# A linear-attention block beside a bilinear feed-forward: four tiles centred first and scaled late, and another order of loads

## The chip, the cores and the metric

The kernel runs on one core of one Trainium2 chip. A core has five engines that run their own instruction queues in order and meet through semaphores: TensorE (PE, matrix products), VectorE (DVE), ScalarE (ACT), GpSimd (POOL) and SyncE (SP, which here only issues DMA). The metric is device time of one execution in microseconds, the median of several runs.

## The reference

The input x has 2048 rows of 512. Each row is normalised without learned parameters, and two branches read the result. Branch A is linear attention with 32 heads of 16: the feature map of queries and keys is the softmax of a per-head 16x16 projection, joined with the softmax of its negative. Branch B multiplies two projections elementwise and projects back. Everything is bfloat16.

```python
xn = (x - mean(x)) / sqrt(var(x) + 1e-5)
q, k, v = heads(xn @ wqkv)
pq, pk = q @ w_phi[h], k @ w_phi[h]              # 16 x 16 for each head
phi = lambda p: concat([softmax(p), softmax(-p)])
kv, z = phi(pk).T @ v, sum_s phi(pk)
o = (phi(pq) @ kv) / (phi(pq) @ z + 1e-6)
A = concat_heads(o) @ wo
B = ((xn @ w_gate) * (xn @ w_up)) @ w_down
out = x + A + B
```

## The kernel before

The 2048 rows are 16 tiles of 128 (index t), the 512 columns four quarters (q), the 1792 hidden columns 14 tiles (ft), and the rows of the feed-forward four groups of 512 (g).

The kernel doesn't write instructions directly. It records steps, each with its engine, what it reads and writes, and an estimated cost; `_order` then simulates the engines with these costs and lays down the order of each engine's queue, and `_emit_all` puts in the semaphore waits. For a DMA the recorded `at` is the time at which its landing is assumed. Steps marked `urgent` go ahead of others that could start at nearly the same time. So a changed cost or `at` may move any later instruction on any engine.

What is recorded, in order:

- Loads, all issued from SP's queue (line 165; transposing loads line 164): x tiles 0, 1, then 2-3 together; wv, the value part of wqkv; x tiles 4-7; the first four hidden tiles of w_gate and of w_up (`load_gu`, each 512 KB); w_phi; the key part of wqkv transposed (`load_wT(1)`); x tiles 8-15; the rest of the weights.
- 46 matmuls of zeros into PSUM bank 7, which wait for no load (line 369).
- For tiles 0 to 3 one after the other, `ln(t, 1)` and `k_pe(t)`. `ln` takes statistics of the tile (DVE, lines 413 and 415), adds epsilon (line 420, on DVE for the first four tiles, on POOL after) and raises to -0.5 on POOL (line 422); `emit_xn` subtracts the mean and scales (DVE, line 437), and for tiles below 8 transposes the tile with four 128x128 matmuls, which ACT copies out of PSUM into xnT. Tiles 8 to 15 are transposed by DMA. `k_pe` multiplies xnT with wv (a group of four 128x512 matmuls, "value group"), and ACT copies the result to vext.
- `make_wbd` spreads w_phi to block-diagonal form on POOL (line 395); `wprime(1)` multiplies it with the transposed key weights, 16 matmuls of 128x128, into the folded weights Wp.
- Then tiles in fours: `k_pk` (four matmuls with Wp, "key group") and `emit_exp`: ACT copies the scores and their negative side by side (1024 columns), DVE takes a tree of maxima (line 477) and subtracts (483), ACT exponentiates; `k_norm` sums on DVE (497) and normalises (521, 524). Between them go units of the feed-forward, `glu(g, ft)`: a gate group, an up group, ACT copies the gate, DVE multiplies (line 548) into hT. An up group reuses a PSUM bank that an earlier unit's DVE product must have read, and a gate group one that ACT must have read; with three banks the two kinds alternate.
- `emit_kv` multiplies keys and values; then the query side (`q_pk`, `q_scale`, `q_T`, `q_num`; `q_num` divides on DVE, line 618); and `final(t)`, 18 matmuls of 128x512 for the output tile, to which DVE adds x (line 645) before it is stored.

The helpers `mms` (line 297, all matmuls) and `act_op` (line 277, all ACT work) record for all others, so many different operations share those two lines.

Of the kernel before, what the change touches and what calls it, by code (L numbers as in the profile page):

```python
# [20 lines left out]
NQ = D // 128  # L21
# [176 lines left out]
def _build(nc, es, A_x, A_wqkv, A_w_phi, A_wo, B_w_gate, B_w_up, B_w_down, out):  # L198
# [93 lines left out]
    def mms(items, prio=None, warm=False):  # L292

        def fn(e):
            ins = None
            for o, l, r, a, z in items:
                ins = e.matmul(o, lhsT=l, rhs=r, start=a, stop=z)  # L297
            return ins
        reads = []
        writes = []  # L300
        c = 0.0
        for o, l, r, a, z in items:
            reads += [l, r]
            writes.append(o)
            c += max(25.0, o.free_size() / 2.4 + 2.3) * (1.6 if warm else 1.0)
        return sc.step(PE, fn, reads=reads, writes=writes, cost=c, lat=260.0, prio=prio)
# [33 lines left out]
    def load_w(on, dst, src, at, issue=500.0):  # L340
        return sc.dma(on, dst, src, at=at, issue=issue)
# [5 lines left out]
    def load_gu(on, f0, n, at):  # L347
# [4 lines left out]
    load_x(SP, 0, 1, 3150.0)  # L352
    load_x(SP, 1, 1, 3700.0)
    load_x(SP, 2, 2, 4800.0)
    load_w(SP, wv_v, A_wqkv[:, 1024:1536].rearrange("(q p) j -> p q j", p=128), 6800.0)
    load_x(SP, 4, 4, 8200.0)
    load_gu(SP, 0, 4, 10800.0)
    sc.dma(SP, wphi_v, bass.AP(tensor=A_w_phi.tensor, offset=A_w_phi.offset, ap=[[16, 128], [2048, NQ], [1, 16]]),
           at=12500.0)
    load_wT(1, 14500.0)  # L360
    load_x(SP, 8, 8, 17000.0)
# [7 lines left out]
    mms([(bank(7, 0, 128), zero, zero, True, True)] * 46, warm=True)  # L369
# [39 lines left out]

    def emit_ln_stats(t0, n):  # L410
# [3 lines left out]
        for t in range(t0, t0 + n):  # L414
# [4 lines left out]
        add = dve if t0 < 4 else pool  # L419
        add(lambda e: e.tensor_scalar(out=veps.unsqueeze(2), in0=var4, scalar1=1e-5, scalar2=None, op0=ALU.add),  # L420
            [mv_v[:, ts, :]], [veps], n)
# [13 lines left out]

    def emit_xn(t):
# [7 lines left out]
        b = next_a()  # L444
        mms([(bank(b, q * 128, 128), xn_tile(t)[:, q * 128:(q + 1) * 128], ident, True, True) for q in range(NQ)])
        act_op(xnT_v[:, :, t * 128:(t + 1) * 128], bank(b).rearrange("p (q s) -> p q s", q=NQ))
# [17 lines left out]
    def emit_exp(src_bank, e_out):  # L464
# [5 lines left out]
        act_op(pst[:, 0:512], bank(src_bank))  # L470
        act_op(pst[:, 512:1024], bank(src_bank), scale=-1.0)
# [35 lines left out]
    def k_pe(t):  # L507
        b = next_a()
        mms(group(bank(b), [(xnT(q, t * 128, 128), wv_v[:, q, :]) for q in range(NQ)]))
        act_op(vext_all[:, t, :, 0:64], bank(b).rearrange("p (c j) -> p c j", c=8))  # L510

    def k_pk(t):
        b = next_a()
        mms(group(bank(b), [(xnT(q, t * 128, 128), Wp_v[:, 1, q, :]) for q in range(NQ)]))
        p_slot["k", t] = emit_exp(b, ek_v[:, t, :])
# [74 lines left out]
    def q_pk(t):  # L590
        b = next_q()
        mms(group(bank(b), [(xnT(q, t * 128, 128), Wp_v[:, 0, q, :]) for q in range(NQ)]))
        p_slot["q", t] = emit_exp(b, eq(t))
# [18 lines left out]
    def q_num(t):  # L612
# [5 lines left out]
        dve(lambda e: e.tensor_tensor(  # L618
            out=o.rearrange("p (g h d) -> p g h d", g=8, h=4),
            in0=nd[:, :, 0:64].rearrange("p g (h d) -> p g h d", h=4),  # L620
            in1=w[:, :, :, None].to_broadcast([128, 8, 4, 16]), op=ALU.mult),
            [nd[:, :, 0:64], w], [o], 512)
# [8 lines left out]
    def final(t, b, cols=(0, 512)):  # L631
# [13 lines left out]
        dve(lambda e: e.tensor_tensor(out=og, in0=ob, in1=xs, op=ALU.add), [ob, xs], [og], c1 - c0, prio=-2.0)  # L645
# [17 lines left out]
    for t in range(4):  # L663
        first = len(sc.steps)
        ln(t, 1)
        for st in sc.steps[first:]:
            st.urgent = True
        k_pe(t)
    make_wbd()
    wprime(1)  # L670
# [191 lines left out]
```

## Time and profile before

| | us |
|---|---|
| median of three runs (223.28 to 223.78) | 223.43 |
| profiled execution | 222.97 |
| its span, first to last instruction | 221.2 |
| PE busy | 215.5 |
| DVE busy | 191.8 |
| ACT busy | 116.1 |
| POOL busy | 9.1 |
| matmuls of zeros and tile 0's transposes, in a row | 1.04 to 5.74 |
| PE idle before tile 1's transposes; before tile 3's | 0.72; 0.44 |
| first transposing load on SP's queue, issue | 5.19 to 11.11 |
| tiles 8-15 used first on DVE | 17.39 |

A row of the timeline gives start and length, engine, line, operation and shapes, how many instructions were merged into it (x), and in brackets the idle time of the engine before it with what ended that. A matmul's recorded length (some 380 ns for 512 columns) includes its run through the array; the next one starts before it has ended, so the pace is read from how many start in a stretch. About one matmul record in fifty is missing. Times below are in microseconds from the start of the span.

### The profile page before, as it was taken

The numbers are of one execution on the slowest core, as the hardware profiler recorded it, in microseconds if no ns is written. First come the engines' busy times: TensorE is split into PE (matmuls) and PEld (weight loads), VectorE is DVE, ScalarE is ACT, GpSimd is POOL, SyncE is SP. The second block draws the span as 40 slices with busy tenths as digits, with TensorE's granted clock in tenths as the row PEclk, the third lists the DMA queues.
The fourth block names the chain that finished last, engine by engine and source line by source line (L and its number), as shares of the span: only waits on it lengthen the run. The fifth ranks groups of instructions, "written<-read, shape, count | busy, mean of one in ns | idle before, by whom it ended". The sixth has DMA issues, their size and how long they took to land.

```text
span 221.2 us, 3597 instructions
## 1 busy us (share of the span) xinstructions
PE 215.5 (97%) x1288; PEld 107.1 (48%) x1312; DVE 191.8 (87%) x552; ACT 116.1 (52%) x193; POOL 9.1 (4%) x25
## 2 busy tenths in 40 slices
PE   8799999999999999999999999999999999999995
PEld 8355444444455454444464445444445444445444
DVE  5858999999992899999998999999999999985121
ACT  2769977684535999655527855646643331300000
POOL 4252000000020000000000000000000000000000
PEclk9999999999999999999999999999999999999999
DMA  5999941300005400000000044464245546745201
GB/s 172 328 281 401 357 128 28 71 0 0 0 9 91 95 3 0 0 0 3 0 1 3 0 82 84 49 139 77 53 94 118 119 98 101 160 94 123 71 24 49
DMA packets 44210, 19.39 MB, mean 88 GB/s; under 512 B 35232, under 2 KB 43168, under 8 KB 44192
## 3 DMA queue, kind: packets, MB, share of 16 engines
q1 hardware_dynamic: 44192, 19.16, 35.7%
q8 instruction: 10, 0.16, 0.3%
q14 instruction: 8, 0.07, 0.1%
HBM read 8.67 MB, written 2.10 MB: 49 GB/s over the span
## 4 chain that ended last, share of the span: by engine, by line
PE 73%; DVE 16%; SPq 4%; DMA 3%; issue 2%
PE ps L297 73%; DVE arena L548 4%; DVE arena L497 3%; DMA arena<-in_A_x_dram 3%; SPq L164 3%; DVE arena L477 3%; SPq L165 2%; DVE arena L413 2%; DVE arena L483 2%; DVE arena L521 1%; DVE arena L524 1%; DVE arena L437 0%; DVE arena L645 0%; DVE arena L415 0%
## 5 line engine op out<-in xcount | busy, mean ns | idle before, releaser
L297 PE MATMUL ps<-arena 128*128 128x512 bf16 (+4 forms) x1288 | 215.5, 328 | 3.5 <-DVE arena L368 1.0
L297 PEld LDWEIGHTS ps<-arena 128*128 128x128 bf16 x1312 | 107.1, 99 | 111.7 <-DVE arena L420 1.3
L277 ACT ACTIVATE arena<-ps 128x512 bf16<-128x512 f32 (+1 forms) x160 | 84.6, 596 | 47.3 <-PE ps L297 44.1
L277 ACT ACTIVATE arena<-arena 128x1024 bf16<-128x1024 bf16 x32 | 34.1, 1069 | 29.3 <-DVE arena L483 28.8
L497 DVE TENSOR_TENSOR arena<-arena 128x256 f32<-128x256 f32 (+3 forms) x128 | 48.8, 392 | 0.1
L548 DVE TENSOR_TENSOR arena<-ps,arena 128x512 bf16<-128x512 f32 x56 | 37.7, 674 | 2.8 <-ACT arena L277 1.4
L477 DVE TENSOR_TENSOR arena<-arena 128x256 bf16<-128x256 bf16 (+3 forms) x128 | 30.6, 267 | 2.9 <-ACT arena L277 2.8
L645 DVE TENSOR_TENSOR arena<-ps,arena 128x512 bf16<-128x512 f32 (+2 forms) x17 | 11.1, 655 | 13.8 <-PE ps L297 13.7
L483 DVE TENSOR_TENSOR arena<-arena 128x1024 bf16<-128x1024 bf16 x32 | 21.5, 671 | 0.0
L413 DVE BATCH_NORM_STATS2 arena<-arena 128x6 f32<-128x512 bf16 x16 | 10.6, 682 | 2.9 <-DMA arena<-in_A_x_dram 2.9
L618 DVE TENSOR_TENSOR arena<-ps,arena 128x512 bf16<-128x512 f32 x16 | 10.9, 680 | 0.1
L524 DVE TENSOR_TENSOR arena<-arena 128x1024 bf16<-128x1024 bf16 x16 | 10.8, 676 | 0.0
L521 DVE RECIPROCAL arena<-arena 128x64 bf16<-128x64 f32 x16 | 8.7, 541 | 0.0
L437 DVE TENSOR_SCALAR arena<-arena 128x512 bf16<-128x512 bf16 x16 | 6.1, 404 | 1.5 <-issue 1.5
L604 DVE TENSOR_TENSOR arena<-arena 128x512 bf16<-128x512 bf16 x16 | 6.5, 409 | 0.0
L617 DVE RECIPROCAL arena<-ps 128x32 f32<-128x32 f32 x16 | 5.5, 343 | 1.1 <-PE ps L297 1.1
L601 DVE RECIPROCAL arena<-arena 128x32 f32<-128x32 f32 x16 | 5.5, 343 | 0.0
L422 POOL TENSOR_TENSOR arena<-arena 128x1 f32<-128x1 f32 (+1 forms) x7 | 5.3, 764 | 4.1 <-DVE arena L420 3.9
L602 DVE TENSOR_TENSOR arena<-arena 128x32 bf16<-128x32 f32 x16 | 2.8, 173 | 0.0
L420 POOL TENSOR_SCALAR arena<-arena 128x4 f32<-128x4 f32 x3 | 0.7, 227 | 50.3 <-DVE arena L415 50.3
L415 DVE BATCH_NORM_AGGREGATE arena<-arena 128x2 f32<-128x6 f32 x16 | 1.9, 160 | 0.1
L571 DVE SCALAR_TENSOR_TENSOR arena<-arena 128x4 bf16<-128x4 bf16 x8 | 1.7, 218 | 0.0
(19 smaller groups left out, 9.6 us busy)
## 6 DMA issues: line engine op xcount, KB each, us to landing
out_dram<-arena SPq DMA_DIRECT2D x15, 128.0 KB, 1.9
arena<-in_B_w_down_dram SPq DMA_DIRECT2D x1, 1792.0 KB, 17.4
arena<-in_B_w_gate_dram SPq DMA_DIRECT2D x1, 1280.0 KB, 8.9
arena<-in_B_w_up_dram SPq DMA_DIRECT2D x1, 1280.0 KB, 12.8
arena<-in_A_x_dram SPq DMA_DIRECT2D x1, 1024.0 KB, 6.2
arena<-arena SPq DMA_TRANSPOSE x40, 2.9
arena<-in_A_wqkv_dram SPq DMA_DIRECT2D x1, 512.0 KB, 4.3
arena<-in_A_x_dram SPq DMA_DIRECT2D x1, 512.0 KB, 5.5
```

The source lines that it names most:

```text
L164: return e.dma_start_transpose(out_ap, in_ap)
L277: return e.activation(out=out_ap, in_=in_ap, func=func, scale=scale, **kw)
L297: ins = e.matmul(o, lhsT=l, rhs=r, start=a, stop=z)
L413: dve(lambda e, t=t: e.bn_stats(stats_v[:, t, 0:6], x_tile(t)), [x_tile(t)], [stats_v[:, t, 0:6]], 512)
L477: dve(lambda e, dst=dst, src=src, k=k: e.tensor_tensor(out=dst, in0=src[:, :, 0:k], in1=src[:, :, k:2 * k], op=ALU.max), [src], [dst], 16 ...
L483: dve(lambda e: e.tensor_tensor(out=p4, in0=p4, in1=src[:, :, None, :].to_broadcast([128, 16, 16, 4]), op=ALU.subtract), [pst, src], [pst] ...
L497: dve(lambda e, dst=dst, src=src, k=k: e.tensor_tensor(out=dst, in0=src[:, :, 0:k], in1=src[:, :, k:2 * k], op=ALU.add), [src[:, :, 0:2 * ...
L521: dve(lambda e: e.reciprocal(out=rs, in_=sm), [sm], [rs], 64, rate=6.0)
L524: dve(lambda e: e.tensor_tensor(out=e4, in0=e4, in1=r4[:, :, None, :].to_broadcast([128, 16, 16, 4]), op=ALU.mult), [ek_v[:, t, :], rs], [ ...
L548: dve(lambda e: e.tensor_tensor(out=dst, in0=bank(bu), in1=gr, op=ALU.mult), [bank(bu), gr], [dst], 512, prio=-1.0)
L618: dve(lambda e: e.tensor_tensor(out=o.rearrange("p (g h d) -> p g h d", g=8, h=4), in0=nd[:, :, 0:64].rearrange("p g (h d) -> p g h d", h= ...
L645: dve(lambda e: e.tensor_tensor(out=og, in0=ob, in1=xs, op=ALU.add), [ob, xs], [og], c1 - c0, prio=-2.0)
```

## The change

Tiles 0 to 3 (`RAW = 4`) are no longer scaled before they are transposed: DVE subtracts the mean alone, and xnT holds centred values for these 512 rows. The scale 1/sqrt(var+eps) is applied where it is needed later: ACT applies it when it copies values and scores out of PSUM (`scale_of`), the product of the feed-forward, which has the scale twice, is multiplied by 1/(var+eps) in the last addition (`scalar_tensor_tensor` in `final`), and the attention output, which must not have it, is multiplied by (var+eps) in `q_num`. For tile 1 the mean comes from ACT, a Copy with a sum over the row, and the statistics for its scale are taken on DVE after tile 3. The adds of epsilon for the first four tiles move from DVE to POOL.

Tile 0 is transposed and copied in two halves, and its value group waits for each half. There are 28 matmuls of zeros instead of 46, and three more after tile 0's transposes; their planned cost is 1.92 instead of 1.6 times a full-speed matmul's.

The wv load moves from SP's queue to ACT's, ahead of ACT's first work. On SP the x tiles 2 and 3 become two loads, and the first gate and up weights go ahead of x tiles 4-7. Several assumed landings change.

In the laid-down order: on PE, tile 1's transposes come ahead of value group 0; tile 4's transposes, which stood between the second unit's two groups, now follow the third unit with those of tiles 5 and 6, and tile 7's follow key group 0. On POOL, the four adds and powers of tiles 0 to 3 and the block-diagonal build come ahead of the add and power of tiles 4 to 7, which before stood ahead of the build. The gate group of unit 8 stands ahead of the up group of unit 4.

```diff
-            c += max(25.0, o.free_size() / 2.4 + 2.3) * (1.6 if warm else 1.0)
+            c += max(25.0, o.free_size() / 2.4 + 2.3) * (1.92 if warm else 1.0)
...
-    load_x(SP, 0, 1, 3150.0)
-    load_x(SP, 1, 1, 3700.0)
-    load_x(SP, 2, 2, 4800.0)
-    load_w(SP, wv_v, A_wqkv[:, 1024:1536].rearrange("(q p) j -> p q j", p=128), 6800.0)
-    load_x(SP, 4, 4, 8200.0)
-    load_gu(SP, 0, 4, 10800.0)
+    load_x(SP, 0, 1, 3050.0)
+    load_w(ACT, wv_v, A_wqkv[:, 1024:1536].rearrange("(q p) j -> p q j", p=128), 5200.0)
+    load_x(SP, 1, 1, 3600.0)
+    load_x(SP, 2, 1, 4300.0)
+    load_x(SP, 3, 1, 4900.0)
+    load_gu(SP, 0, 4, 8400.0)
+    load_x(SP, 4, 4, 9900.0)
     sc.dma(SP, wphi_v, ...
-           at=12500.0)
-    load_wT(1, 14500.0)
-    load_x(SP, 8, 8, 17000.0)
+           at=10200.0)
+    load_wT(1, 12200.0)
+    load_x(SP, 8, 8, 16500.0)
...
-    mms([(bank(7, 0, 128), zero, zero, True, True)] * 46, warm=True)
+    mms([(bank(7, 0, 128), zero, zero, True, True)] * 28, warm=True)
...
+    def emit_moments(t):
+        dve(lambda e: e.bn_stats(stats_v[:, t, 0:6], x_tile(t)), [x_tile(t)], [stats_v[:, t, 0:6]], 512)
+        dve(lambda e: e.bn_aggr(mv_v[:, t, :], stats_v[:, t, 0:6]), [stats_v[:, t, 0:6]], [mv_v[:, t, :]], 6)
+
+    def emit_centred(t):
+        mean = mv_v[:, t, 0:1]
+        if t == 1:
+            mean = lnt_v[:, 2, 8:9]
+            sc.step(ACT, lambda e: e.activation(out=bank(6), in_=x_tile(t), func=ACTF.Copy, scale=1.0 / 512.0,
+                                                accum_out=mean),
+                    reads=[x_tile(t)], writes=[bank(6), mean], cost=600.0, lat=180.0)
+        else:
+            emit_moments(t)
+        dve(lambda e: e.tensor_scalar(out=xn_tile(t), in0=x_tile(t), scalar1=mean, scalar2=None, op0=ALU.subtract),
+            [x_tile(t), mean], [xn_tile(t)], 512, rate=0.5)
+
+    def emit_root(t):
+        pool(lambda e: e.tensor_scalar(out=veps(t), in0=mv_v[:, t, 1:2], scalar1=1e-5, scalar2=None, op0=ALU.add), ...
+        pool(lambda e: e.tensor_tensor(out=rstd_v[:, t, 0:1], in0=veps(t), in1=mhalf[:, 0:1], op=ALU.pow), ...
+
+    def emit_squares():
+        dve(lambda e: e.reciprocal(out=lnt_v[:, 2, 0:RAW], in_=lnt_v[:, 0, 0:RAW]), ...
+
+    def scale_of(t):
+        return rstd_v[:, t, 0:1] if t < RAW else 1.0
...
-        add = dve if t0 < 4 else pool
-        add(lambda e: e.tensor_scalar(out=veps.unsqueeze(2), in0=var4, ...
+        pool(lambda e: e.tensor_scalar(out=veps.unsqueeze(2), in0=var4, ...
...
-        act_op(pst[:, 0:512], bank(src_bank))
-        act_op(pst[:, 512:1024], bank(src_bank), scale=-1.0)
+        act_op(pst[:, 0:512], bank(src_bank), scale=scale_of(t))
+        act_op(pst[:, 512:1024], bank(src_bank) if t >= RAW else pst[:, 0:512], scale=-1.0)
...
-        mms(group(bank(b), [(xnT(q, t * 128, 128), wv_v[:, q, :]) for q in range(NQ)]))
-        act_op(vext_all[:, t, :, 0:64], bank(b).rearrange("p (c j) -> p c j", c=8))
+        items = group(bank(b), [(xnT(q, t * 128, 128), wv_v[:, q, :]) for q in range(NQ)])
+        for part in ((items[0:2], items[2:4]) if t == 0 else (items,)):
+            mms(part)
+        act_op(vext_all[:, t, :, 0:64], bank(b).rearrange("p (c j) -> p c j", c=8), scale=scale_of(t))
...
+        if t < RAW:
+            dve(lambda e: e.scalar_tensor_tensor(out=o4, in0=n4, scalar=veps(t), in1=w4, op0=ALU.mult, op1=ALU.mult),
+                [nd[:, :, 0:64], veps(t), w], [o], 512)
+            return
...
+        if t < RAW:
+            r2 = lnt_v[:, 2, t:t + 1]
+            dve(lambda e: e.scalar_tensor_tensor(out=og, in0=ob, scalar=r2, in1=xs, op0=ALU.mult, op1=ALU.add),
+                [ob, r2, xs], [og], c1 - c0, prio=-2.0)
...
-    for t in range(4):
+    for t in range(RAW):
         first = len(sc.steps)
-        ln(t, 1)
+        emit_centred(t)
+        emit_T(t, 2 if t == 0 else 1)
         for st in sc.steps[first:]:
             st.urgent = True
+        if t == 0:
+            mms([(bank(7, 0, 128), zero, zero, True, True)] * 3, warm=True).deps.append(sc.by_eng[PE][-2])
+        if t == 1:
+            emit_moments(t)
+        emit_root(t)
         k_pe(t)
     make_wbd()
+    emit_squares()
     wprime(1)
```

## The prediction, made before the changed kernel was run

> **What bounds the kernel now.** I read the page first (which engine is full), then the timeline of the opening (what ends each idle time of that engine), then busy time by stretches, then the landings of the loads. From the page's table of engines:
>
> ```profile
> PE 215.5 (97%) x1288; PEld 107.1 (48%) x1312; DVE 191.8 (87%) x552; ACT 116.1 (52%) x193; POOL 9.1 (4%) x25
> ```
>
> TensorE (PE) is busy 97% of a span of 221.2 us; the profiled execution took 222.97, the median of the runs is 223.43. A gain must come from where PE does not do useful work. The timeline (start, duration, engine, line, in brackets the idle time before) shows where:
>
> ```profile
> 1.04 4.70 PE L297 MATMUL ps<-arena 128*128 128x128 bf16 x50 [1.04 <-DVE arena L368]
> ...
> 2.19 0.47 SPq L165 DMA_DIRECT2D arena<-in_A_wqkv_dram  x1
> ...
> 3.00 0.69 DVE L413 BATCH_NORM_STATS2 arena<-arena 128x6 f32<-128x512 bf16 x1 [0.80 <-DMA arena<-in_A_x_dram]
> 3.73 0.18 DVE L415 BATCH_NORM_AGGREGATE arena<-arena 128x2 f32<-128x6 f32 x1
> 3.95 0.15 DVE L420 TENSOR_SCALAR arena<-arena 128x1 f32<-128x1 f32 x1
> 4.19 0.56 POOL L422 TENSOR_TENSOR arena<-arena 128x1 f32<-128x1 f32 x1 [2.04 <-DVE arena L420]
> 4.84 0.38 DVE L437 TENSOR_SCALAR arena<-arena 128x512 bf16<-128x512 bf16 x1
> 5.77 0.60 ACT L277 ACTIVATE arena<-ps 128x512 bf16<-128x512 f32 x1 [3.70 <-PE ps L297]
> 6.46 2.44 PE L297 MATMUL ps<-arena 128*128 128x128 bf16 x15 [0.72 <-DVE arena L420]
> 8.27 0.69 DVE L413 BATCH_NORM_STATS2 arena<-arena 128x6 f32<-128x512 bf16 x1 [0.56 <-DMA arena<-in_A_x_dram]
> 8.88 0.40 DVE L437 TENSOR_SCALAR arena<-arena 128x512 bf16<-128x512 bf16 x1
> 9.33 22.90 PE L297 MATMUL ps<-arena 128*128 128x128 bf16 x130 [0.44 <-DVE arena L437]
> 11.74 1.05 POOL L422 TENSOR_TENSOR arena<-arena 128x4 f32<-128x4 f32 x1
> 12.89 0.89 DVE L437 TENSOR_SCALAR arena<-arena 128x512 bf16<-128x512 bf16 x2 [1.55 <-issue]
> 17.39 1.88 DVE L413 BATCH_NORM_STATS2 arena<-arena 128x6 f32<-128x512 bf16 x3 [1.53 <-DMA arena<-in_A_x_dram]
> 31.34 0.62 DVE L548 TENSOR_TENSOR arena<-ps,arena 128x512 bf16<-128x512 f32 x1
> ```
>
> 46 of the first 50 matmuls multiply zeros. Real work begins with tile 0's transposes (about 5.35) and stutters to 9.33, each time behind a normalised tile (L437); from 9.33 PE has no gap to its end. From 9.33 it runs T3 (transposes of tile 3) and the value groups v2 and v3, so the first gate group starts near 11.3.
>
> ```profile
> 1.22:4.64 3.42, 3.42 (x35) 3.42 (x33) 1.85 (x5) 0.85 (x1) 1.36 (x6) 1.00 0.69 184
> 4.74:5.52 0.78, 0.78 (x17) 0.78 (x15) 0.78 (x4) 0.00 (x0) 0.17 (x2) 1.00 1.09 373
> ...
> 18.26:38.12 19.86, 19.75 (x92) 8.97 (x92) 19.86 (x56) 16.75 (x30) 1.27 (x2) 1.00 0.66 221
> ```
>
> Columns: stretch, length, then busy us (instructions) of PE, PEld, DVE, ACT, POOL, granted clock, DMA share, GB/s. Two readings. A 128-wide matmul takes 3.42/33 = 0.104 us up to 4.64 and 0.78/15 = 0.052 us after 4.74: the array ran at half speed until 4.7, although the clock column says 1.00. And from 18.26 to 38.12 PE starts a 512-wide matmul every 19.86/92 = 0.216 us while VectorE (DVE) is busy all 19.86 us: two full engines.
>
> The loads, by another such table, and time from issue to landing:
>
> ```profile
> 1.75:3.00 1.25, 1.25 (x15) 1.25 (x13) 0.29 (x1) 0.32 (x1) 0.38 (x3) 1.00 0.80 216
> 3.00:3.50 0.50, 0.50 (x8) 0.50 (x6) 0.50 (x1) 0.00 (x0) 0.00 (x0) 1.00 0.39 53
> ...
> 4.25:4.75 0.50, 0.50 (x8) 0.50 (x7) 0.47 (x2) 0.00 (x0) 0.50 (x1) 1.00 0.98 221
> 4.75:10.00 5.25, 4.04 (x38) 2.31 (x38) 4.62 (x16) 3.11 (x6) 1.66 (x3) 1.00 1.07 361
> ```
> ```profile
> arena<-in_A_wqkv_dram SPq DMA_DIRECT2D x1, 512.0 KB, 4.3
> arena<-in_B_w_up_dram SPq DMA_DIRECT2D x1, 512.0 KB, 7.5
> ```
>
> wv is issued at 2.19 and lands at 6.5; the first up weights are issued at 3.80 and land at 11.3. The engines move 361 GB/s once fed, but 216, 53 and 221 in three early stretches, when SP's one queue has no rows ready.
>
> **The change, part by part.**
>
> *Scale taken off the path.* Tile 0's xn was ready at 5.22 (4.84+0.38): statistics, aggregate, add, POOL power, subtract-and-scale. Now the subtraction follows the aggregate at 3.95 and ends at 4.33: 0.89 us earlier. The powers still run (POOL 0.56 each) behind the value matmuls; they gate only value evacuations, and v0's is wanted near 6.2, so they cost nothing there. Tile 1's mean comes from ACT: its form is not in the trace; bounds 0.60 (a PSUM-reading 128x512 ACTIVATE) and 1.07 (the 128x1024). I take 0.6; ACT has only its table load (1.28 us, behind the wv issue of about 0.47, ended near 2.6) ahead of it. With x1 landing at 3.4 to 3.7 the mean is there at 4.1 to 4.4, just when DVE ends tile 0; at 1.07 all later tiles shift 0.4.
>
> *DVE's chain through four tiles.* Subtract 1 starts at 4.35. Then per tile: statistics to aggregate 0.73, aggregate to subtract 0.22, subtract to next 0.32, so 1.27. Subtract 3 ends at 4.35+0.32+2x1.27-0.32+0.38 = 7.27, against 9.28. T3 takes 0.22, v2 and v3 8x0.216 = 1.73: first gate at 7.3+1.95 = 9.3, 9.4 with a tenth for slower x landings. Against 11.3 that is 1.9. Matters that must hold: v0 needs wv (below) and tile 0's evacuation, whose two halves end at about 5.1 and 5.5 (two of 0.38, estimated between a 128x65's 0.225 and 0.60); v0, T2, v1 then fill 5.2 to 7.2, just before T3.
>
> *wv beside the x tiles.* SP issues eight loads before the transposing one in both kernels, so nothing on SP moves earlier; wv is issued near 0.8 on ACT instead of 2.19. Bounds for its landing: 6.5 (no gain; first gate then 10.4) and about 0.8+4.3 = 5.1. I take 5.2: x0 to x3 and wv are 1 MB, 2.8 us at 361 GB/s from 1.8. Tiles x1 to x3 may each slip some tenths; DVE wants x2 at 4.7 and x3 at 5.9, so only x0 and x1 cost one for one. The Trainium skill, "DMA: Bandwidth & Descriptors", section "Issuing engines are not separate DMA queues", says that issuing from several engines saves sequencer time alone, since the same 16 engines interleave; by that wv would gain only its 1.4 us of earlier issue. The trace shows unfilled stretches that a second queue can fill, and where both end is nearly the same 5.1.
>
> *x4 to x7 moved behind gate and up.* This is given back. The bytes up to and with them are those up to and with the up weights before (11.3). The three slow stretches lack (361-216)x1.25+(361-53)x0.5+(361-221)x0.5 = 405 KB, 1.1 us. So x4-7 land between 10.2 (all filled) and 11.3 (none); I take 10.3, against 8.2. Behind it on DVE: three statistics 1.8, one product 0.6, the fourth 0.6, four aggregates 0.45, then add and power on POOL, 1.55 as from 11.34 to 12.89, then three xn 1.05: T6 can go at 10.3+6.1 = 16.4 and the first key group k0 behind it at 16.6. PE alone would be there at 9.4+3.45 (two gate-up units)+0.9 (folded weights)+1.73 (third unit)+0.67 (T4 to T6) = 16.15. So x4-7 set it. Before, k0 started at 9.33+0.22+1.73+16x0.216+0.22+0.9+1.73+0.67 = 18.26; after it T7 (0.22) still comes. Gain: 18.26-16.6-0.22 = **1.4 us**. The folded weights wait for their own transposing load, 2.0 behind up before, so about 12.4, before PE needs it at 12.85; gate (7.4) and up (8.9) land before 9.4 and 10.3.
>
> *POOL's order.* The block-diagonal build (1.83 us in all, waiting for w_phi) now stands ahead of tiles 4-7's add and power. w_phi lands about 0.2 behind x4-7, so POOL is free at 12.4, while the aggregates end at 13.75: covered by 1.3 us.
>
> *DVE from 18 to 65.* DVE is full there, so PE's lead must not outrun it. DVE's first key tree starts at x4-7 plus 9.45 (6.35 to the end of tile 7's xn, product 0.6, four statistics 2.42, aggregate) = 19.75, 3.15 behind k0. Adding the matmuls up to each group that waits for a DVE product, and DVE's rows up to that product, in the new order, the tightest allows 3.3 and most 3.6 to 4.4; the old order allowed 3.0 and had 2.98 (the product of 31.34 ended 0.1 before its waiter). So no new stall, by 0.2 us. ScalarE's second half of the exponent input now reads the first half: same count, same sizes.
>
> *Late scaling.* Eight 128x512 DVE operations get a second operand. The trace has that form only with 4 columns, 0.218 us, as a 128x64 TENSOR_TENSOR's 0.218; bounds 0 and 0.4 each (an extra 128x512 pass, L437). Even 3.2 us lie in a stretch where DVE is idle some 16 of 105 us. I take 0. Fifteen zero matmuls fewer: they end at 1.04+28x0.104 = 3.95, before T0 at 4.4; no cost if the speed-up still comes at 4.7.
>
> Sum: 222.97-1.4 = 221.6 for a profiled execution, **222.0** against the median.
>
> **Rivals.**
>
> *A, the loads are not filled in* (one set of engines serves both queues, and the gaps merely move). x4-7 land at 11.3; k0 at 17.6; gain 0.4: 223.0. For it: nothing shows a second queue; against: the three gaps.
>
> *B, the clock; ends slower.* What raised the speed at 4.7 followed 3.66 us of unbroken matmuls. The new burst breaks at 3.95, is resumed at 4.4, and has small holes until 7.3. If the array stays at half speed, PE itself bounds the opening: 8.9 us of half-speed work from T0 to v3 starting at 4.4. Released at time c, the first gate is at c/2+6.7: 10.7 for c = 8.1 (3.66 us counted anew from 4.4; gain 0.5, 222.9), 12.4 for 11.5 (counted from a last hole near 7.8; loss 1.2, **224.6**); even at c = 9.2. Against it: in before the speed outlived pauses of 0.9 and 0.6 us, though that is keeping, not gaining. The Trainium skill, "TensorE: Matmul & The Clock Gate", section "Part 1: The HAM clock gate (the "warmup" mystery)", asks for about 3.4 us of sustained activity in a free-running window, and 28 zero matmuls last less; read strictly, that is this rival, read as mostly busy, the forecast. The trace's 3.66 us agrees with the length.
>
> *C, DVE becomes the bound.* The margin of 0.2 us is gone if DVE meets 0.7 us of new waits on ACT before 65 us; PE then stalls the missing 0.5: gain 0.9, 222.5. For it: DVE full 18 to 65; against: the new order puts one more gate group ahead of the tight products.
>
> **How the numbers follow.** Forecast 0.57, A 0.17, B 0.18 (0.13 at 224.6, 0.05 at 222.9), C 0.08. The likeliest gives 222.0, its own range 221.4 to 222.6 (x4-7 at 10.1 to 10.8, some lost tenths). Leaving a tenth on each side: 221.2 to 223.2. 0.2% is 0.45 us, about what a measurement tells from no change. Faster: 0.57+0.08+half of A and of B's mild form = 0.76; same: the other halves, 0.11; slower 0.13.
>
> **What would show it.** Right: tile 0's subtraction ends by 4.5; 128-wide matmuls at 0.05 to 0.06 from 4.8; wv in by 5.5; T3 near 7.3 to 7.5, first gate near 9.4; x4-7 in near 10.3 and a PE wait of some tenths before T5 or T6; no PE gap after. Wrong: x0 later than 3.5, 0.10 us pitches past 5, x4-7 after 10.8, or PE waiting for DVE products between 25 and 65.

## The result, and the profile after

The changed kernel is slower, not faster. It was measured on three occasions, each time beside the kernel before:

| | median, us | ratio to before | 95% interval |
|---|---|---|---|
| first (7 executions, 224.28 to 226.53; before 223.38) | 225.80 | 1.0096 | 1.0069 to 1.0122 |
| again, run e9 (11 executions, 222.90 to 225.60; before 223.29) | 224.05 | 1.0027 | 1.0002 to 1.0052 |
| again, run e13 (before 223.31) | 224.64 | 1.0049 | 1.0021 to 1.0077 |

So the loss is 0.3 to 1.0%, and the kernel varies more than the one before it. The forecast was 222.0. Single executions far slower than the rest (387 to 1316 us, one each in e13, e14 and e15; 227.10 in e2; 228.44 and 228.51 in e7) count in the medians but not in the ratios. The first profiled execution took 224.98, with a span of 223.3 against 221.2; the median execution lost 0.8 more and has no profile. PE's work is the same but for 15 zero matmuls fewer:

```profile
PE 216.4 (97%) x1273; PEld 107.0 (48%) x1297; DVE 192.7 (86%) x549; ACT 117.5 (53%) x196; POOL 10.6 (5%) x29
```

All but some 0.3 of the 2.0 us (the spans unrounded) is lost in the first 13 us. The timeline of the changed kernel (start, length, engine, line, operation; in brackets the idle time before it and what ended it):

```profile
0.78 0.45 ACTq L165 DMA_DIRECT2D arena<-in_A_wqkv_dram  x1
...
1.04 3.17 PE L297 MATMUL ps<-arena 128*128 128x128 bf16 x28 [1.04 <-DVE arena L369]
...
4.09 0.35 DVE L427 TENSOR_SCALAR arena<-arena 128x512 bf16<-128x512 bf16 x1
...
4.50 0.61 PE L297 MATMUL ps<-arena 128*128 128x128 bf16 x4 [0.30 <-DVE arena L427]
...
5.83 0.60 ACT L422 ACTIVATE ps<-arena 128x512 f32<-128x512 bf16 x1 [3.29 <-DMA arena<-in_A_x_dram]
6.37 0.19 ACT L422 ACTIVATION_READ_ACCUMULATOR ps<-arena 128x1 f32 x1
...
6.66 0.35 DVE L427 TENSOR_SCALAR arena<-arena 128x512 bf16<-128x512 bf16 x1 [2.22 <-ACT ps L422]
...
7.08 7.17 PE L297 MATMUL ps<-arena 128*128 128x128 bf16 x35 [1.97 <-DVE arena L427]
```

Tile 0 goes as forecast: its subtraction ends at 4.44, its transposes start at 4.50. Then ACT waits 3.29 us for x1, which lands at 5.81 instead of 3.35; DVE waits 2.22 for ACT's mean, and PE 1.97 for DVE. The transposes that stood at 6.46 before stand at 7.08. The three zeros that the change adds after tile 0's transposes stand in PE's laid-down order behind tile 1's, so they bridge nothing and take 0.32 us there. The second loss shows in the stretches after that (busy us and instructions of PE, PEld, DVE, ACT, POOL, granted clock, DMA share, GB/s):

```profile
7.10:10.30 3.20, 3.20 (x16) 1.88 (x17) 3.02 (x9) 1.15 (x2) 1.95 (x4) 1.00 1.11 341
10.90:13.00 2.10, 2.10 (x13) 0.96 (x13) 1.88 (x3) 1.28 (x4) 1.64 (x5) 1.00 1.14 239
```

16 matmuls (11 of 128 columns, 5 of 512) share 3.20 us of unbroken work in the first stretch, 13 (4 and 9) share 2.10 in the second: a 512-wide one starts 0.427 after the one before it, later 0.216, while the clock column says 1.00 in both. The array is at half speed until 10.4 to 10.8; before, it was released at 4.7. The first gate group starts at 13.0 instead of 11.3. The loads that the change moved:

```profile
arena<-in_A_wqkv_dram ACTq DMA_DIRECT2D x1, 512.0 KB, 4.7
arena<-in_A_x_dram SPq DMA_DIRECT2D x4, 128.0 KB, 4.4
```
```profile
1.75:3.00 1.25, 1.25 (x14) 1.25 (x13) 0.29 (x1) 0.79 (x1) 0.37 (x3) 1.00 0.56 152
3.00:3.50 0.50, 0.50 (x8) 0.50 (x6) 0.35 (x1) 0.00 (x0) 0.00 (x0) 1.00 0.47 137
3.50:4.25 0.75, 0.70 (x7) 0.44 (x5) 0.68 (x3) 0.00 (x0) 0.10 (x1) 1.00 1.06 363
4.25:4.75 0.50, 0.24 (x3) 0.25 (x4) 0.20 (x1) 0.00 (x0) 0.42 (x2) 1.00 1.09 383
```

wv, issued at 0.78, lands at 5.44 (6.50 before), and the four single x tiles need 4.4 from issue to landing: x1 to x3, issued behind wv's rows, land at 5.81, 6.16 and 6.52. The gap near 4.5 is filled (383 against 221 GB/s), but the first stretch is poorer (152 against 216): by 4.75 the engines had moved 152x1.25+137x0.5+363x0.75+383x0.5 = 722 KB, against 659 KB before by the same sum (336 GB/s from 3.5 to 4.25). In this pair of profiles the second queue gave 63 KB, where the forecast had 405. Over all profiles read here the sum is 722 to 836 KB with wv issued at 0.78 on ACT's queue, and 580 to 714 with every load on SP's or wv issued late.

The view of the DMA queues (queue, packets, MB, share) shows why x1 is late. q1 holds SP's loads, q10 the wv load from ACT. From 1.75 to 3.00, then from 3.00 to 4.25:

```profile
q1 hardware_dynamic: 144, 0.13, 36.7%
q10 hardware_dynamic: 57, 0.06, 19.4%
```
```profile
q10 hardware_dynamic: 333, 0.34, 82.4%
```

In the second stretch q1 moves nothing; before, it moved 0.28 MB there. The two queues did not share the engines then: SP's stood while ACT's was served.

### The profile page after: what moved, and what is told of

The parts are those of the page before. It is cut to its first block, busy times and chain, and to the rows that moved or that the text cites. A ratio compares the mean times of both kernels' runs of the same rounds, so it can differ in the third digit from the quotient of the medians.

```text
span 223.3 us, 3574 instructions
## 1 busy us (share of the span) xinstructions
PE 216.4 (97%) x1273; PEld 107.0 (48%) x1297; DVE 192.7 (86%) x549; ACT 117.5 (53%) x196; POOL 10.6 (5%) x29
## 4 chain that ended last, share of the span: by engine, by line
PE 95%; DMA 2%; issue 1%; ACT 0%; DVE 0%; SPq 0%; DVEq 0%
PE ps L297 95%; DMA arena<-in_A_x_dram 2%; ACT ps L422 0%; SPq L165 0%; DVE arena L427 0%; DVE arena L697 0%; DVEq L880 0%
## 5 line engine op out<-in xcount | busy, mean ns | idle before, releaser
L277 ACT ACTIVATE arena<-ps 128x512 bf16<-128x512 f32 (+2 forms) x141 | 74.8, 590 | 40.3 <-PE ps L297 35.6
L277 ACT ACTIVATE arena<-arena 128x1024 bf16<-128x1024 bf16 (+1 forms) x40 | 39.2, 993 | 30.2 <-DVE arena L525 30.1
L539 DVE TENSOR_TENSOR arena<-arena 128x512 f32<-128x512 bf16 (+3 forms) x128 | 49.1, 393 | 0.1
L592 DVE TENSOR_TENSOR arena<-ps,arena 128x512 bf16<-128x512 f32 x56 | 37.9, 677 | 3.6 <-PE ps L297 3.4
L519 DVE TENSOR_TENSOR arena<-arena 128x64 bf16<-128x64 bf16 (+3 forms) x128 | 31.7, 267 | 4.5 <-ACT arena L277 4.1
L697 DVE TENSOR_TENSOR arena<-ps,arena 128x512 bf16<-128x512 f32 (+2 forms) x13 | 8.4, 646 | 9.1 <-PE ps L297 9.1
L568 DVE TENSOR_TENSOR arena<-arena 128x1024 bf16<-128x1024 bf16 x16 | 10.9, 679 | 0.0
L277 ACT ACTIVATE arena<-ps,arena 128x512 bf16<-128x512 f32 x12 | 7.9, 694 | 4.8 <-PE ps L297 4.8
L669 DVE TENSOR_TENSOR arena<-ps,arena 128x512 bf16<-128x512 f32 x12 | 8.2, 682 | 0.1
L457 POOL TENSOR_TENSOR arena<-arena 128x4 f32<-128x4 f32 x3 | 3.1, 1042 | 0.2
```

The lines of the kernel that those rows point to most:

```text
L277: return e.activation(out=out_ap, in_=in_ap, func=func, scale=scale, **kw)
L519: dve(lambda e, dst=dst, src=src, k=k: e.tensor_tensor(out=dst, in0=src[:, :, 0:k], in1=src[:, :, k:2 * k], op=ALU.max), [src], [dst], 16 ...
L539: dve(lambda e, dst=dst, src=src, k=k: e.tensor_tensor(out=dst, in0=src[:, :, 0:k], in1=src[:, :, k:2 * k], op=ALU.add), [src[:, :, 0:2 * ...
L568: dve(lambda e: e.tensor_tensor(out=e4, in0=e4, in1=r4[:, :, None, :].to_broadcast([128, 16, 16, 4]), op=ALU.mult), [ek_v[:, t, :], rs], [ ...
L592: dve(lambda e: e.tensor_tensor(out=dst, in0=bank(bu), in1=gr, op=ALU.mult), [bank(bu), gr], [dst], 512, prio=-1.0)
L669: dve(lambda e: e.tensor_tensor(out=o4, in0=n4, in1=w4, op=ALU.mult), [nd[:, :, 0:64], w], [o], 512)
```

## The experiments

A ledger holds the profiles on which the argument rests. From the first key group on, PE has hardly a gap, so a span differs from that of before (221.2) by where that group starts, plus, in the new order alone, tile 7's transposes (0.22) that follow it, plus later waits of PE. Times are us from the span's start; "full" is when the matmuls' pace doubles; group starts are counted out in the laid-down order with missing records filled in.

| profile | x1 | full | tile 1 | first gate | first key group | later waits | span |
|---|---|---|---|---|---|---|---|
| before | 3.35 | 4.7 | 6.46 | 11.29 | 18.26 | 0 | 221.2 |
| changed | 5.81 | 10.4-10.8 | 7.08 | 13.01 | 19.75 | 0.25 | 223.3 |
| changed again (e9) | 5.22 | 9.3 | 6.49 | 12.15 | 18.89 | 0.19 | 222.3 |
| e5, before, 28 zeros | 3.36 | see below | 6.38 | 12.21 | 19.18 | 0.70 | 222.9 |
| e4, before, wv on ACT's queue | 5.82 | 6.1 | 8.29 | 12.78 | 19.74 | 0 | 222.7 |
| e1, changed, 46 zeros | 5.43 | 5.5 | 6.69 | 11.12 | 17.87 | 1.27 | 222.4 |
| e14, changed, 56 zeros | 5.43 | 4.1 | 6.69 | 11.12 | 17.87 | 0.17 | 221.3 |
| e3, wv on SP's, 46 zeros | 3.36 | 4.5 | 5.46 | 11.09 | 17.83 | 1.29 | 222.4 |
| e6, wv ahead of x2 | 3.45 | 6.7 | 6.35 | 10.93 | 17.87 | 0 | 221.1 |
| e11, and x4-7 first | 3.50 | 5.1 | 5.75 | 10.81 | 17.81 | 0.18 | 221.2 |

For the changed kernel: 19.75+0.22-18.26+0.25 = 1.96 of the 2.0. The other rows close to 0.12 or better.

**The clock: e1, e5, e14.** The burst of zeros is lengthened in the changed kernel, or shortened in the kernel before, with the planned costs kept, so that every queue's order stays (46 in e1, 56 in e14; e5 sets 28 in the kernel before).

```diff
-    mms([(bank(7, 0, 128), zero, zero, True, True)] * 28, warm=True)
+    mms([(bank(7, 0, 128), zero, zero, True, True)] * 46, warm=True).cost = 28 * (128 / 2.4 + 2.3) * 1.92
```

> The changed kernel with 46 zero matmuls again instead of 28 (the order of every queue as in the changed kernel; x1 still lands at about 5.8). Theory L+C (x1's late landing makes a hole before tile 1's transposes, and the short first burst then leaves the array at half speed until about 3.6 us after the restart): the long burst brings full speed at about 4.7, it survives the hole, tile 0's transposes start near 5.4 instead of 4.5, tile 1's still near 7.1, the 0.10 us pitches are gone after 4.7, the first gate group starts near 11.5 instead of 13.0, and the time is 223.3 to 223.6. Rival H (the hole itself sets the clock back, whatever stood before it): full speed at 4.7, half speed again from 7.1 to about 10.6, first gate group near 13, about 225.5. Rival K (the clock has little to do with the loss, the loads' new order sets it): first gate earlier but the time within 0.5 of the changed kernel's.

Measured: 223.97, ratio 1.0015 (0.9994 to 1.0036). Full speed at 5.5, kept through a hole of 0.8 (rival H falls); the first gate group at 11.12. The time is 0.4 above the expected one, by a later wait of 1.1 that is treated below, and beside e9's 224.05 rival K would still stand; e14 decides it.

> The kernel before with 28 zero matmuls instead of 46, and nothing else (all loads and orders as before). Theory C (a burst of 2.9 us ends before the speed is raised, which in the long bursts seen so far came 3.5 to 5 us after the first matmul or later; then the count starts anew with real work): 0.10 us pitches still after 5.4, half speed until somewhere between 8.5 and 12, the first gate group at 11.7 to 13 instead of 11.3, a median of 224.0 to 225.5, and executions that differ by 1 us or more. Rival (mostly busy is enough): full speed by about 5, time within 0.3 of the kernel before.

Measured: 224.83, ratio 1.0061 (1.0037 to 1.0085); executions from 223.97 to 225.42. Eighteen zeros fewer, and nothing else, cost the old kernel 1.4 us. By the ledger 0.92 of its profile's 1.62 is lost in the opening and 0.70 in later waits. Its stretches:

```profile
5.10:5.50 0.40, 0.30 (x4) 0.23 (x4) 0.40 (x3) 0.00 (x0) 0.22 (x1) 1.00 0.95 338
...
7.60:10.50 2.90, 2.90 (x14) 1.52 (x14) 2.35 (x6) 1.68 (x4) 0.55 (x1) 0.50 1.18 336
11.00:13.00 2.00, 2.00 (x11) 0.90 (x10) 0.45 (x5) 1.19 (x2) 1.56 (x3) 1.00 1.08 254
```

The way was another one than expected: tile 0's four transposes at 5.2 do run at full speed, and the speed is taken away again at about 7.4, after 3.4 us (4.05 to 7.46) in which PE was busy for 1.63, idle from 4.2 to 5.2 and from 5.6 to 6.4; it comes back at 10.9. Here the clock column shows it (0.50). The trace's record of the granted clock has the first grant at 4.05, the withdrawal at 7.46 and the return at 10.87, 3.41 apart each.

> The changed kernel with 56 zero matmuls instead of 28, nothing else: they last until about 5.9, or 6.9 if the speed comes late, and tile 1's transposes can't start before 6.5 to 7.0 because of x1. Theory C: at full speed from tile 1's transposes on in the profile, first gate group near 11 to 11.5, median 0.7 to 1.5 below the changed kernel's on this chip and a range of 1.5 us or less. Rival (the loss is the loads alone): median within 0.3 of the changed kernel's. By the fetch theory no wait above 0.1 before a q_num either.

Measured: 223.39, ratio 1.0008 (0.9990 to 1.0026), while the unaltered kernel (e13) had 224.64 and 1.0049 on that chip: 1.25 us by medians, 0.9 by ratios. Its stretches show 28 starts in 2.90 at half speed and 31 in 1.50 from 4.2 on:

```profile
1.10:4.00 2.90, 2.90 (x28) 2.90 (x29) 0.92 (x2) 1.28 (x1) 1.02 (x5) 1.00 0.60 172
4.20:5.70 1.50, 1.50 (x31) 1.50 (x29) 0.43 (x2) 0.25 (x1) 0.96 (x2) 1.00 1.08 355
```

One edit of a number gives back the time of the kernel before, and nothing more, and the ledger puts the difference into the opening (first key group at 17.87 instead of 19.75) although x1 is as late as ever. The changed kernel was also run unaltered:

> The changed kernel once more, unaltered: its executions range over 2.2 us and the one profiled is faster than the median, so a second profile and more times are wanted. Theory C (half speed after the short burst, released or withdrawn at moments that the program does not set): tile 1's transposes at half speed again, the release somewhere between 8 and 14, median 225 to 226, range 2 us or more. Rival: half speed was an accident of one execution, the second profile runs at full speed from 4.7 to 7.1 on and its time is near 223.5.

> The changed kernel, unaltered, as the common reference on this chip: 223.8 to 225.8 median, range 2 us or more, tile 1's transposes at half speed unless this execution is one of those where the speed comes early.

Their times are in the table above; e9's median of 224.05 is below the 225 to 226 expected, e13's is in its range. e9's profile again has tile 1 at half speed; the 512-wide matmuls that start at 9.34 and 9.55 already have the full pace, so the release came at 9.3 (the change of the granted clock is recorded at 9.32). e13's profiled execution is the one of 387 us and is not read.

**The hole: e10, e12.** Does filling the pause ahead of tile 1 help without a longer first burst?

```diff
-            mms([(bank(7, 0, 128), zero, zero, True, True)] * 3, warm=True).deps.append(sc.by_eng[PE][-2])
+            fill = mms([(bank(7, 0, 128), zero, zero, True, True)] * 23, warm=True)
+            fill.cost = 3 * (128 / 2.4 + 2.3) * 1.92
+            fill.deps.append(sc.by_eng[PE][-2])
```

> The changed kernel with 23 instead of 3 zero matmuls behind tile 0's transposes (28 ahead of them as in the changed kernel, wv on ACT's queue, x1 late as there), so that PE is busy from 4.5 until x1's transposes near 7.0. Theory C: with the hole of 2.2 us filled the speed is raised between 4.5 and 7.4, tile 1 and all behind it run at full speed, first gate group near 11.5, 223.3 to 224.3 as in the first experiment. Rival S (only an unbroken first burst counts, and the short one is lost whatever follows): half speed still beyond 7.4, 225 or more.

Measured: 225.92, ratio 1.0108 (1.0080 to 1.0136). The edit did not do what it was meant to: the planner laid the added zeros behind tile 1's transposes (27 matmuls in one row, with the pause still ahead), so it tells nothing of the hole. The 20 needless matmuls take 2.1 us there at half speed (20x0.107), and the profile (227.01, the slowest execution) has a later wait besides, 1.24 at 191.9.

```profile
6.50 3.06 PE L297 MATMUL ps<-arena 128*128 128x128 bf16 x27 [1.38 <-DVE arena L427]
```

With a dependency the zeros were put ahead of tile 1:

```diff
+        if t == 1:
+            sc.by_eng[PE][-1].deps.append(bridge)
...
+            bridge = mms([(bank(7, 0, 128), zero, zero, True, True)] * 16, warm=True)
...
```

> The changed kernel with 19 zero matmuls between tile 0's and tile 1's transposes on PE (in the tenth run the added ones stood behind tile 1's, where they only lengthened the opening; here tile 1's transposes are made to follow 16 added ones, and the 3 that were there stand ahead too). 28 zeros ahead of tile 0 as in the changed kernel, wv on ACT's queue, x1 late as there. PE is then busy from 1.04 to 3.95 and from about 4.4 to 6.9. Theory C (a stretch of some 3.4 us, placed by nothing in the program, must be mostly busy): the speed is raised between 4.5 and 8, earlier than in both profiles of the changed kernel (10.4 to 10.8 and 9.5 to 10.0), first gate group near 11.5 to 12, 223.3 to 224.5. Rival S (only an unbroken first burst counts): half speed to 8.5 and beyond, 225 or more.

Measured: 224.38, ratio 1.0067 (1.0042 to 1.0093). In the profiled execution, the fastest with 223.62, the speed had come by 4.34, ahead of the added zeros, which then ended at 5.6 and left a hole all the same:

```profile
4.30:5.60 1.30, 1.26 (x23) 1.26 (x23) 0.00 (x0) 0.00 (x0) 0.65 (x2) 1.00 1.08 368
```

So 28 zeros sometimes do suffice. As the speed came ahead of the added zeros, this profile doesn't part theory C from rival S, and bridging the hole isn't shown to help: its interval overlaps the changed kernel's.

**The load of wv: e4, e2, e3, e7.** First alone, in the kernel before:

```diff
+    load_w(ACT, wv_v, A_wqkv[:, 1024:1536].rearrange("(q p) j -> p q j", p=128), 6800.0)
     load_x(SP, 1, 1, 3700.0)
     load_x(SP, 2, 2, 4800.0)
-    load_w(SP, wv_v, A_wqkv[:, 1024:1536].rearrange("(q p) j -> p q j", p=128), 6800.0)
```

> The kernel before with one edit: the wv load issued from ACT's queue ahead of its first work (46 zeros, scaling at once, all other loads and orders as before). Theory L: x1 lands near 5.8 instead of 3.35, tile 1's xn is ready near 8.0, the first gate group starts near 12.4 instead of 11.3, and the time is about 1 us longer, 224.2 to 224.7, although wv itself lands 1 us earlier. Rival (the second queue only fills gaps): x1 before 4.2, time within 0.4 of the kernel before.

Measured: 225.33, ratio 1.0074 (1.0048 to 1.0101). x1 lands at 5.82, as expected, and the cost is larger than expected:

```profile
5.84 0.69 DVE L413 BATCH_NORM_STATS2 arena<-arena 128x6 f32<-128x512 bf16 x1 [1.55 <-DMA arena<-in_A_x_dram]
...
7.11 0.40 PE L297 MATMUL ps<-arena 128*128 128x128 bf16 x4 [0.98 <-DVE arena L420]
```

In DVE's queue the statistics of tile 1 stand ahead of tile 0's scaling, so tile 0's transposes, too, wait for x1: 7.11 instead of 5.35. In all seven profiles read here in which wv is issued at 0.78 on ACT's queue x1 lands at 5.2 to 5.8; in all others at 3.3 to 3.9. In each of the seven SP's queue moves 0.01 MB or less from 3.00 to 4.25. Then wv was put back on SP's queue behind x3 in the changed kernel, without (e2) and with (e3) the longer burst:

```diff
-    load_w(ACT, wv_v, A_wqkv[:, 1024:1536].rearrange("(q p) j -> p q j", p=128), 5200.0)
...
     load_x(SP, 3, 1, 4900.0)
+    load_w(SP, wv_v, A_wqkv[:, 1024:1536].rearrange("(q p) j -> p q j", p=128), 5200.0)
```

> The changed kernel with the wv load back on SP's queue, behind x3 (28 + 3 zeros and every order else as in the changed kernel). Theory L+C: x1 lands again near 3.4, tile 1's subtraction ends near 4.8, no hole of 2 us; wv lands near 6.0 to 6.5. What the clock does after the short burst is open: full speed near 4.7 gives a first gate group near 9.6 and 222.2; full speed some 3.6 us after 4.4, near 8.1, gives 222.9; full speed only near 11 gives a first gate group near 12.2 and 224.5. Rival (x1 was late for another reason than wv's rows ahead of it): x1 still after 5, and the time within 0.5 of the changed kernel's.

> Both edits: wv on SP behind x3, and 46 zeros. Theory L+C: full speed at 4.7, x1 near 3.4, tile 0's transposes at 5.4, no 0.10 us pitch after 4.7, first gate group near 10.0, DVE's chain still early, 222.0 to 222.4. Rival D (late scaling with the gate and up weights ahead of x tiles 4-7 costs on its own, by waits of PE for T5 or for DVE's key trees): first gate group near 10 but PE idle later, 223.0 or more.

Measured: e2 225.07, ratio 1.0059 (1.0026 to 1.0092), executions from 223.22 to 227.10; e3 223.80, ratio 1.0018 (0.9996 to 1.0041). x1 is back at 3.9 and 3.4. With 28 zeros that mends nothing reliably: in the profiled execution, the slowest (227.10), wv came only at 8.3 and full speed at 13.5. With 46 the loss is gone, but the forecast's gain doesn't appear. Two lines of profiles tell why. In e3 PE stands before the first value group, for wv, which lands at 6.93:

```profile
7.06 8.14 PE L297 MATMUL ps<-arena 128*128 128x512 bf16 x49 [1.05 <-DMA arena<-in_A_wqkv_dram]
```

and PE waits another 1.11 before q_num of tile 11; e1 shows the same in its chain of waits (start, length, what):

```profile
184.28 4.70 DMA arena<-arena
188.98 0.05 issue
189.03 3.02 PE ps L297 x20
```

The transposing transfer of that tile's query features (the store that the expectations speak of) took 4.70 from issue to landing, where most take 3.0 to 3.3. PE waits for this transfer in e7 and e10 too (0.61 and 1.24 idle). In the new order the reserve between its landing and q_num is 0.46 in the changed kernel's profile, against 1.29 before. e3's kernel with wv issued later, on ACT's queue:

```diff
+    first_act = act_op(bank(6, 0, 128), zero)
...
+    late = load_w(ACT, wv_v, A_wqkv[:, 1024:1536].rearrange("(q p) j -> p q j", p=128), 5200.0)
+    late.deps.append(first_act)
```

> The third experiment's kernel with wv on ACT's queue, but behind a small first ACT operation, so that it is issued near 2.4 and not at 0.78, after the four x loads of SP's queue. Theory Q (rows are served in the order in which they were issued, on whatever queue): x1 to x3 stay at 3.4 to 4.6, wv lands at 6.4 to 6.9, hardly earlier than from SP, first gate group near 10.7 to 11.1, time within 0.4 of the third run's. Rival (ACT's queue is served ahead of SP's, whatever was issued first): x2 and x3 slip past 5 and wv lands near 5.5.

Measured: 225.08, ratio 1.0058 (1.0028 to 1.0087). Issued at 2.40, wv leaves x1 to x3 alone (3.28 to 4.67) but lands at 7.50, and PE waits for it until 7.63: theory Q in kind, and worse in size (its time was to be within 0.4 of e3's 223.80).

**Other orders of the opening: e6, e11.** On SP's queue x0, x1, wv, x2, x3; then also x tiles 4-7 ahead of the gate and up weights; both with 46 zeros. Of e6 and of e11:

```diff
     load_x(SP, 1, 1, 3600.0)
+    load_w(SP, wv_v, A_wqkv[:, 1024:1536].rearrange("(q p) j -> p q j", p=128), 5200.0)
     load_x(SP, 2, 1, 4300.0)
     load_x(SP, 3, 1, 4900.0)
```
```diff
+    load_x(SP, 4, 4, 9900.0)
     load_gu(SP, 0, 4, 8400.0)
-    load_x(SP, 4, 4, 9900.0)
```

> The third experiment's kernel (46 zeros, all loads on SP's queue) with the wv load moved ahead of x2 and x3: x0, x1, wv, x2, x3. In the third run PE stood 1.21 us before value group 0, which waited for wv (6.93). Theory W (wv is the next late item): wv lands near 5.5 to 6.0, x2 near 6.2 and x3 near 6.6, value group 0 starts near 5.9; now DVE's chain through x2 and x3 sets the end, subtract 3 at about 8.6, first gate group near 10.5 instead of 11.1, 0.4 to 0.6 less than the third run's. Rival: what is won there is only waited for later (transposed query features or x tiles 4-7), time within 0.2 of the third run's.

> The sixth experiment's kernel (46 zeros, SP's queue with x0, x1, wv, x2, x3) with x tiles 4-7 ahead of the first gate and up weights again. In the sixth run PE waited 0.1, 0.1 and 0.1 us for tiles 4 to 7. Theory W: x4-7 land near 8.0, gate near 9.6, up near 11.2, just ahead of the first up group; those waits go; first gate group at 10.4 to 10.9; 0.2 to 0.4 us less than the sixth run's, a median of 223.3 to 223.7, no better than the kernel before where a fetch of instructions falls on a transposing store of the query features. Rival G (the late up weights cost what x4-7 give back): PE waits before the first up group and the time is the sixth run's or longer.

Measured: e6 223.85, ratio 1.0018 (1.0002 to 1.0035); e11 223.33 beside 223.29, ratio 1.0016 (0.9993 to 1.0038). The 0.4 to 0.6 that e6 was to win over e3 did not come. wv lands at 5.7 and 5.9, and now x3 is last (6.44 and 6.64). In e11 the first up group waits 0.25 for its weights (11.87), as rival G has it. Run again beside e16, e11's kernel (e15) had 1.0025 (1.0001 to 1.0048) and a median above the expected 223.9. None of these kernels beats the one before.

**Fetches of instructions: e8, e15, e16.** In e1 and e3 a 16 KB packet of the instruction queue falls on that slow transfer (the queues in the stretch from 184.1 to 185.8 of e1: packets, MB, share):

```profile
q1 hardware_dynamic: 384, 0.19, 40.7%
q8 instruction: 1, 0.02, 5.3%
```

5.3% of 16 engines over 1.7 us is one engine for 1.45. Fewer or more zero matmuls shift where PE's fetches fall: twelve wide ones in e3's kernel (e8), 56 instead of 46 in e11's (e16).

```diff
-    dve(lambda e: e.memset(zero, 0.0), [], [zero], 128)
-    mms([(bank(7, 0, 128), zero, zero, True, True)] * 46, warm=True).cost = 28 * (128 / 2.4 + 2.3) * 1.92
+    dve(lambda e: e.memset(sbv("tree", 0, 512), 0.0), [], [sbv("tree", 0, 512)], 128)
+    wide = sbv("tree", 0, 512)
+    mms([(bank(7), zero, wide, True, True)] * 12, warm=True).cost = 28 * (128 / 2.4 + 2.3) * 1.92
```

> The third experiment's kernel with 12 zero matmuls of 512 columns instead of 46 of 128: the same length of burst at half speed (5.1 against 4.9 us), but 34 matmuls fewer in PE's instruction stream, so that each later fetch of 16 KB of instructions comes about 7 us later relative to the work (in the runs with 46 zeros one of 1.5 us fell on the transposing store of the features of tile 11, at 184.2, and PE waited 1.1 us for them at 187.9). Theory F (that wait is this collision): the wait of 1.1 us before q_num of tile 11 is gone and the time is 222.7 to 223.2, unless the fetch falls on another of these transfers. Rival (the wait is the new order's too short distance between DVE's scaling and q_num): it stays at 1.1 and the time at 223.8.

Measured: 225.53, ratio 1.0092 (1.0076 to 1.0107). The wait before tile 11's q_num is gone; new ones stand before a key-value product (0.78, at 72.0), where ACT waits for a transposing transfer, and before q_num of tiles 4 and 8 (0.73 and 0.54), whose transfers took 4.5 and 4.3.

> The eleventh run's kernel again (46 zeros, x0, x1, wv, x2, x3, x4-7, gate, up on SP's queue), as the reference on this chip: 223.3 to 223.9 median; by the fetch theory a part of its executions, not all, has a wait of about 1 us before q_num of tile 11.

> The same with 56 zeros. Theory F (a fetch of 16 KB of PE's instructions delays a transposing store that it falls on): each fetch comes 10 matmuls, 2.2 us, earlier, and lies in the gaps of the query side's transposing stores (near 182.2, 159.6 and 141.3 by the sixth run's positions); no wait above 0.1 before any q_num, median 222.6 to 223.1, 0.3 to 0.8 below the run with 46 zeros and below the kernel before. Rival (the order's short reserve alone): the same time as with 46 zeros, within 0.2.

Measured: e15 224.11, e16 224.27, ratio 1.0027 (0.9998 to 1.0056). Neither profile has a wait before a q_num, so they don't part the theories, and the forecast of 0.3 to 0.8 less fell: e16 waited 0.57 for the transposed key weights instead, and its full speed came at 6.3. That such transfers sometimes take 4 to 5 us and that the new order has less reserve for it is seen. No run moved a fetch alone, but the 17 profiles taken together (all but e13's) speak for theory F. They have 337 transposing transfers issued after 130 us that took 2.9 us or more. 204 of them had no instruction packet of 8 KB or more under way in their first 3.0 us, and the longest of these took 3.33; 133 had one, and 54 of those took 3.6 to 5.0. So every slow transfer coincides with a fetch, though not every fetch slows one, and that a fetch causes the delay is likely and not shown by an experiment.

## Why the prediction was wrong

- *Tile 0 without its scale: right.* Subtraction ended at 4.44 (forecast 4.33, and x0 0.15 later than before). ACT's mean took 0.73 with the read of its sum, inside the bounds of 0.6 to 1.07.
- *"Tiles x1 to x3 may each slip some tenths": the first step that failed.* x1 slipped 2.46 us, x3 1.65. The sum took 1 MB (x0 to x3 and wv) at 361 GB/s from 1.8 on, hence 4.6; in the profiles of the table the megabyte is complete at 6.0 to 6.9 whatever its order (in e2, e7, e8 and e15 only at 7.3 to 8.3), and the stretch up to 3.0 stays poor: 131 to 152 GB/s with wv on ACT's queue from 0.78, 207 to 226 without. A second queue put another load first and filled little. The Trainium skill's rule cited then ("DMA: Bandwidth & Descriptors", section "Issuing engines are not separate DMA queues") was the better guide to the gain: wv came 1.06 earlier, less than its 1.4 of earlier issue. Its word that such transfers interleave isn't borne out from 3.00 to 4.25, where SP's queue moved nothing, and the loads behind paid for it.
- *"No cost if the speed-up still comes at 4.7": the second, and the one that sets the sign.* It was rival B's condition. Rival B at c = 11.5 gave 224.6 with the first gate at 12.4; measured c = 10.4 to 10.8, 13.0, and 224.98 for that execution. Its formula took the half-speed work to start at 4.4; x1's lateness let it start at 7.08. The chance of 0.18 was too low: the forecast's condition was that 2.9 us of zeros do what 3.7 us had done in the only profile at hand. Of the six profiles read here with 28 zeros, only e5 and e12 have full speed at tile 0's transposes, and e5 lost it again.
- *x4 to x7 at 10.3: at the late bound.* 11.10 (10.2 to 11.3 were the bounds), and it cost nothing, since PE reached its first key group at 19.75 anyway; in e6, where PE came early, the waits for tiles 5 and 6 were 0.1 each. It would have cost the gain, though: with the prediction's own 6.3 us from this landing to the first key group, 11.10 gives 17.4 and leaves 18.26-17.4-0.22 = 0.64 of the 1.4, even with a perfect opening. That is nearly rival A.
- *DVE's margin of 0.2 us: held, at a slightly smaller lead.* DVE's first key tree starts 2.94 behind the first key group (22.69 and 19.75; 3.15 was forecast, 3.3 allowed). In the changed kernel's profile PE waits 0.17 near 27.9, and nothing else to 65. What the sum didn't look at is the query side, where reserves fell (1.29 to 0.46 for tile 11, 1.56 to 0.6 for tile 8 where its transfer took 3.2).
- *Late scaling: right.* The eight two-operand operations cost 0.06 each more than the one-operand form (0.74 against 0.68), below the bound of 0.4:

```profile
L697 DVE TENSOR_TENSOR arena<-ps,arena 128x512 bf16<-128x512 f32 x11 | 7.5, 686 | 6.4 <-PE ps L297 6.4
L694 DVE SCALAR_TENSOR_TENSOR arena<-ps,arena 128x512 bf16<-128x512 f32 x4 | 3.0, 742 | 0.0
```

- *The 1.4 us of gain: not there even with both mended.* The first gate group was forecast at 9.4 and comes at 10.8 to 11.1 in every mended order. The scale was off the path, but the path had a second limit just behind it, the first megabyte of loads: whichever of wv, x1 or x3 is put last sets the first value groups or DVE's chain. e14's ledger closes at nothing: 17.87+0.22-18.26+0.17 = 0.00.

## What to carry to other kernels

A warm-up burst is a part of the schedule: before shortening it, ask how long the old one ran until the pace of the matmuls doubled, and leave more than that, since the moment varies from run to run (3.1 to 5.6 us here). When a large load is moved to another queue ahead of small ones that gate the start, price what stands behind it, not only the load itself. And where several waits end within a microsecond of each other, take the next one's end as the gain's limit. Here, by the sums above, the first megabyte of loads and the landing of x4 to x7 each took away more than half of the 1.4 us.

## What the runs showed of the hardware

- The doubling of the pace came 3.1 to 5.6 us after the first of an unbroken row of matmuls (4.11 in e14, 6.67 in e6, from 1.04), not at a fixed time, and in e5 it was withdrawn after 3.4 us in which PE was busy for 1.63. The Trainium skill, "TensorE: Matmul & The Clock Gate", section "Part 1: The HAM clock gate (the "warmup" mystery)", tells of a free-running window of about 3.4 us; e5's changes at 4.05, 7.46 and 10.87 fit it. How full a window must be no run here shows, beyond e5's 1.63 being too little.
- In the 17 profiles read here the clock column stayed at 1.00 during the first half-speed phase and showed 0.50 only for the withdrawal in e5, since the record behind it has no entry before the first change (4.71 in the kernel before, none in the changed kernel's profile): the pace of the matmuls is the safer reading.
- A load of 512 KB issued at 0.78 on one queue delayed a 128 KB load issued at 1.25 on another by 1.9 to 2.5 us, while one issued at 0.79 nearly kept its landing (2.9 to 3.3 against 2.8 to 3.0). From 3.00 to 4.25 the other queue moved 0.01 MB or less, the large load 0.34 to 0.46.
- Transposing transfers that mostly take 3.0 to 3.3 us took up to 5.0 where PE waited for them (e10), and 4.84 and 5.01 near 143 us in e3 and e15, where PE didn't wait. Each one of 3.6 us or more that was issued after 130 us coincided with a packet of the instruction queue.
